# Output products in two matmuls of 256 columns, and moving tiles 128 bytes further on

## The chip, the cores and the metric

The kernel runs on one core of a Trainium2 chip. TensorE (PE) multiplies: a weight load puts a stationary tile of 128 columns into the array, and a matmul streams a moving tile of up to 512 columns past it into one bank of PSUM. VectorE (DVE), ScalarE (ACT) and GpSimd (POOL) work beside it, and DMA queues, issued from SyncE (SP) and POOL, move data between HBM and the on-chip memory SBUF. The metric is the time of one execution in device microseconds (us), the median of several runs.

## The reference

```
q = softmax over the 64 channels; k = softmax over the 576 positions     # 8 batches, 8 heads
kv = k^T v                      # per batch and head, 64 x 64
x  = q kv                       # gathered to 4608 tokens x 512
gate = sigmoid(x @ w_gate);  val = x @ w_val          # 512 x 1536 each
out  = (gate * val) @ w_out                           # 1536 x 512
```

All inputs and the output are float32.

## The kernel before, in words

The 4608 tokens are cut into nine windows w of 512. The first (w = 0) runs in plain float32 (lines 613 and 640) while the weights are still being unpacked, and the other eight run in float32r, where every operand is split into a high and a low part and a product is three matmuls: high by high, high by low, low by high.

A window of these eight takes six steps, and a step has two stages on TensorE that follow each other without a gap:

- `g1(w, p)` computes gate and value for 256 of the 1536 inner columns, by a scheme with seven block products of 12 matmuls each: 84 matmuls, all of 256 columns (line 658). Stationary are weights from `a_w` or `s_sb`, moving are the tiles `c_hl`, made from x. Both halves of the array's input are read from SBUF: 128 columns of weights and 256 columns of moving data for each matmul, and each matmul has a weight load of its own.
- `g2(w, at)` multiplies the step before (256 inner columns) by the output weights into four PSUM banks `acc`: 24 matmuls, before the change of 512 columns (line 726). Stationary is `h`, moving is `wo_hl`.

In the steps of each window but the last, the attention of the next window is woven in. Behind the third `g1`, `k_mm` (line 378) makes k^T v for a batch, in 20 float32 matmuls of 128 columns; it follows `g1` and stands ahead of `g2`. Behind the fifth `g2`, `x_mm` (line 541) multiplies q by kv for the four pairs of heads: 3 matmuls for each part of the window, where a window has two parts if a batch ends in it. The parts are 128 and 384 columns in window 2, 192 and 320 in 3, 256 and 256 in 4, 320 and 192 in 5, 384 and 128 in 6, 448 and 64 in 7, and 512 alone in 8. Moving are tiles of the pool `ring`, stationary is `kv_sb`.

The order on every engine is the order in which the code is written (a manual schedule). Where a tile lies in SBUF follows from the order and the sizes of the pools at the top, with unused tiles (`pad_a`, `pad_w`) that push the later pools on. By this allocation the stationary tiles `a_w`, `s_sb`, `h` and `kv_sb` start at 128 bytes modulo 512 in their partition, and the moving tiles `c_hl`, `wo_hl`, `wo_t`, `x_0` and `ring` at 448 modulo 512. Slices inside them are multiples of 512 bytes away from the start, but for the parts in `x_mm`.

The output weights' next pair (`wo_load`, line 234) and the next sums `s_sb` (`s_load`, line 278) are loaded by DMAs on POOL's queue, each as soon as TensorE has read the tile that it overwrites. So TensorE's pace sets when they start.

Of the kernel before, what the change touches and what calls it, by code (L numbers as in the profile page):

```python
# [8 lines left out]
F32 = mybir.dt.float32  # L9
# [8 lines left out]
P = 128  # L18
# [4 lines left out]
HT = T // 2  # L23
NW = NTOK // T
NT = T // P
NP = H // 2
NJ = DF // P
NK = DM // P
NS = NJ // 2
# [22 lines left out]
def attn_moe(ctx: ExitStack, tc: tile.TileContext, qf, qn, qT, k, kT, v, wg, wv, wo, out):  # L52
    nc = tc.nc

    const = ctx.enter_context(tc.tile_pool(name="const", bufs=1))


    cpool = ctx.enter_context(tc.tile_pool(name="cpool", bufs=1))
    apad = ctx.enter_context(tc.tile_pool(name="apad", bufs=1))
    apool = ctx.enter_context(tc.tile_pool(name="apool", bufs=1))  # L60
    two = ctx.enter_context(tc.tile_pool(name="two", bufs=2))
    wpad = ctx.enter_context(tc.tile_pool(name="wpad", bufs=1))
    wpool = ctx.enter_context(tc.tile_pool(name="wpool", bufs=2))
    four = ctx.enter_context(tc.tile_pool(name="four", bufs=4))
    ring = ctx.enter_context(tc.tile_pool(name="ring", bufs=11))
    small = ctx.enter_context(tc.tile_pool(name="small", bufs=2))
    apad.tile([P, 48], F32, name="pad_a")
    wpad.tile([P, 80], F32, name="pad_w")
    dpool = ctx.enter_context(tc.tile_pool(name="dpool", bufs=2, space=bass.MemoryType.DRAM))
    spool = ctx.enter_context(tc.tile_pool(name="spool", bufs=1, space=bass.MemoryType.DRAM))  # L70
    ps_acc = ctx.enter_context(tc.tile_pool(name="ps_acc", bufs=NT, space=bass.MemoryType.PSUM))
# [451 lines left out]
    def x_parts(w):  # L523
        t0 = w * T
        b0, b1 = t0 // S, (t0 + T - 1) // S
        if b0 == b1:
            return [(b0, 0, T)]
        cut = b1 * S - t0
        return [(b0, 0, cut), (b1, cut, T)]

    def x_mm(w, hp):
        qh, ql = qT_hl.pop((w, hp))
        if w > 1 and hp < 3:
            ps = ps_gv.tile([P, T], F32, name="gv")
        else:
            ps = ps_at.tile([P, T], F32, name="at")
        x_ps[w, hp] = ps
        for b, f, t in x_parts(w):
            kh, kl = (kv_sb[:, b % 2, i, hp] for i in range(2))
            for lh, rh in ((0, qh), (0, ql), (1, qh)):  # L540
                nc.tensor.matmul(  # L541
                    ps[:, f:t], lhsT=kl if lh else kh, rhs=rh[:, f:t],
                    start=(lh == 0 and rh is qh), stop=(lh == 1),
                )

    def x_ev(w, hp):
        copy = nc.vector.tensor_copy if hp % 2 and w > 1 else nc.scalar.copy
# [53 lines left out]
    acc = {}  # L601
# [25 lines left out]
    def acc_new(w):  # L627
        acc[w] = [ps_acc.tile([P, DM], F32, name="acc") for _ in range(NT)]

    def acc_out(w):  # L630
        for m in range(NT):
            nc.scalar.copy(out=x_32[:, m], in_=acc[w][m])
            nc.sync.dma_start(out=out[w * T + m * P:w * T + (m + 1) * P], in_=x_32[:, m])
        del acc[w]
# [79 lines left out]
    def step(w, i):  # L714
        return (i - 1) % NS if w == 1 else i

    def g2(w, at):
        p = step(w, at)
        if at == 0:
            acc_new(w)  # L720
        h, o = h_hl.pop((w, p)), wo_hl.pop((w, p))
        for i in range(2):
            for m in range(NT):
                sl = slice(m * P, (m + 1) * P)
                for lh, rh in ((0, 0), (0, 1), (1, 0)):
                    nc.tensor.matmul(  # L726
                        acc[w][m], lhsT=h[lh][:, i, sl], rhs=o[i][:, rh],
                        start=(at == 0 and i == 0 and lh == 0 and rh == 0),
                        stop=(at == NS - 1 and i == 1 and lh == 1),
                    )  # L730
        if at == NS - 1:
            acc_out(w)

# [42 lines left out]
    def side_b(n, p):  # L776
        if p == 0:
            for hp in range(NP):
                q_spread(n, "m", hp)
        if p == 1:  # L780
            for hp in range(NP):
                qT_load(n, hp)
        if p == 2:
            for hp in range(NP):
                q_spread(n, "r", hp)
        if p == 3:
            for hp in range(NP):
                qT_mul(n, hp)
        if p == 4:
            for hp in range(NP):  # L790
                x_mm(n, hp)
                x_ev(n, hp)
            c_subs()
        load_next(n, p)
# [38 lines left out]
    def after_first(j):  # L833
# [28 lines left out]
        if 6 <= j <= 9:  # L862
            x_mm(1, j - 6)
# [76 lines left out]
    ps = ps_acc.tile([P, DM], F32, name="acc")  # L940
# [5 lines left out]
    m = const.tile([P, NP, 1], F32, name="kmax_0")  # L946
# [115 lines left out]
    for w in range(1, NW):  # L1062
        last = w == NW - 1
        for at in range(NS):
            p = step(w, at)
            end = last and at == NS - 1
            g1(w, p, None if end else step(w + (at + 1) // NS, (at + 1) % NS))
            if at == NS - 1 and not last:
                c_split(0)
                h_split(w, p)  # L1070
                for i in range(1, 7):
                    c_split(i)
            else:
                h_split(w, p)
            if not last:
                side_a(w + 1, at)
            if prev is None:
                g2_0(NJ - 1)
                wo_next(1, 0)
                wo_next(1, 1)  # L1080
            else:
                g2(*prev)
                if not end:
                    wo_next(w + (at + 1) // NS, (at + 1) % NS)
            prev = (w, at)
            if not last:
                side_b(w + 1, at)
    g2(*prev)


# [36 lines left out]
```

## Time and profile before

| | |
|---|---|
| median of 3 runs | 973.95 us (973.04 to 975.06) |
| the profiled execution, its own time | 974.03 us |
| its span, first to last instruction | 972.2 us |
| TensorE matmuls busy | 946.6 us, 97% of the span |
| TensorE weight loads busy | 819.3 us, 84% |
| VectorE, ScalarE, GpSimd busy | 613.2, 488.3, 168.3 us |
| mean granted clock of TensorE | 0.991 of full |

The span lies 1.8 us below the profiled execution's own time, and that time is within 0.1 us of the median, so a saving read off the trace can be taken from either. Matmuls overlap in the array, so the "mean" of a group (279 ns for 256 columns) is how long one is under way, not how far apart two follow. How far apart they follow is read from the chain in order of time, where a stage's length divided by its matmuls is the spacing.

### The profile page before, as it was taken

How to read it: one execution, taken by the hardware profiler on the slowest of the kernel's cores; microseconds unless marked ns; L12 is line 12 of the kernel's file. 1: busy time of each engine (PE TensorE's matmuls, PEld its weight loads, DVE VectorE, ACT ScalarE, POOL GpSimd, SP SyncE). 2: the span in 40 equal slices, each digit the busy share in tenths (PEclk: the TensorE clock that was granted, in tenths of full speed). 3: DMA queues.
4: the chain of work that ended last, by engine and by line, in shares of the span. 5: the costliest groups of instructions: out<-in, count | busy, mean ns of one | idle time of the engine just before them, and what ended most of it. 6: DMA issues, size and time to landing. Idle time of an engine off the chain costs nothing.

```text
span 972.2 us, 15629 instructions
## 1 busy us (share of the span) xinstructions
PE 946.6 (97%) x6062; PEld 819.3 (84%) x6062; DVE 613.2 (63%) x1013; ACT 488.3 (50%) x824; POOL 168.3 (17%) x316
## 2 busy tenths in 40 slices
PE   5899998899999999999999999999999999999998
PEld 4444543699999999999999999999999999999997
DVE  8788878766666566756684667566755655564242
ACT  4689784563456354726472547254635333533222
POOL 0110001221112112111211112111212121212210
PEclk8999999999999999999999999999999999999999
DMA  9986475899699978999899979997999689858672
GB/s 326 350 277 256 178 275 201 292 349 322 197 270 341 303 233 208 383 282 274 184 380 309 269 164 382 317 274 155 370 319 250 208 249 311 240 173 258 200 209 71
DMA packets 93865, 257.79 MB, mean 265 GB/s; under 512 B 15264, under 2 KB 17568, under 8 KB 93024
## 3 DMA queue, kind: packets, MB, share of 16 engines
q0 software_dynamic: 43712, 168.32, 57.5%
q1 hardware_dynamic: 50080, 88.48, 31.3%
q8 instruction: 48, 0.79, 0.4%
q14 instruction: 25, 0.20, 0.1%
HBM read 228.20 MB, written 28.56 MB: 264 GB/s over the span
## 4 chain that ended last, share of the span: by engine, by line
PE 91%; DMA 3%; DVE 2%; ACT 2%; issue 1%; POOL 0%; SPq 0%; POOLq 0%; DVEq 0%; ACTq 0%
PE gv L658 48%; PE acc L726 27%; PE gv L613 6%; PE at L378 3%; PE acc L640 3%; PE gv L541 2%; DMA kmax_row<-k_max 1%; DMA s<-s_sb 1%; PE at L541 1%; DMA s_sb<-s 1%; DMA lent<-k_in 1%; ACT s_sb L265 0%; PE acc L564 0%; ACT f_w L162 0%; DVE a_w L269 0%
## 5 line engine op out<-in xcount | busy, mean ns | idle before, releaser
L658 PE MATMUL gv<-c_hl,s_sb 128*128 128x256 f32 x2304 | 284.6, 279 | 0.3 <-DMA s_sb<-s 0.3
L658 PEld LDWEIGHTS gv<-c_hl,s_sb 128*128 128x128 f32 x2304 | 275.7, 188 | 0.4 <-issue 0.4
L726 PE MATMUL acc<-wo_hl,h 128*128 128x512 f32 x1152 | 272.2, 392 | 0.0
L726 PEld LDWEIGHTS acc<-wo_hl,h 128*128 128x128 f32 x1152 | 213.0, 188 | 44.5
L658 PE MATMUL gv<-c_hl,a_w 128*128 128x256 f32 x1728 | 226.2, 279 | 0.7 <-DVE a_w L269 0.7
L658 PEld LDWEIGHTS gv<-c_hl,a_w 128*128 128x128 f32 x1728 | 214.9, 188 | 5.2 <-issue 1.0
L278 POOL DMA_DIRECT2D s_sb<-s x188 | 100.3, 534 | 314.0 <-PE gv L658 313.9
L684 DVE TENSOR_TENSOR sg<-gv,sg 128x512 f32<-128x512 f32 x48 | 33.2, 691 | 148.5 <-PE gv L658 148.3
L676 ACT COPY sg<-gv 128x512 f32<-128x512 f32 x48 | 28.2, 588 | 148.2 <-PE gv L658 146.5
L234 POOL DMA_DIRECT2D wo_hl<-wo x96 | 51.1, 533 | 297.4 <-PE acc L726 297.3
L686 ACT COPY sg<-gv 128x512 f32<-128x512 f32 x48 | 28.2, 587 | 106.2 <-PE gv L658 106.2
L613 PE MATMUL gv<-x,f_w 128*128 128x512 f32 x160 | 72.3, 605 | 3.5 <-ACT h L621 3.5
L688 DVE TENSOR_TENSOR sg<-sg 128x512 f32<-128x512 f32 x48 | 33.2, 693 | 59.8 <-ACT sg L686 59.8
L613 PEld LDWEIGHTS gv<-x,f_w 128*128 128x128 f32 x160 | 30.5, 193 | 41.3 <-issue 35.8
L709 DVE TENSOR_TENSOR h<-sg,h 128x1024 fp32r<-128x1024 f32 x48 | 58.8, 1226 | 1.6
L697 DVE TENSOR_TENSOR sg<-sg 128x512 f32<-128x512 f32 x48 | 33.3, 693 | 33.5 <-ACT sg L691 33.5
L691 ACT ACTIVATE sg<-sg 128x512 f32<-128x512 f32 x48 | 30.4, 632 | 47.9 <-DVE sg L690 47.9
L640 PE MATMUL acc<-wo_t,h 128*128 128x512 f32 x96 | 44.8, 611 | 5.6 <-DVE h L625 5.6
L681 ACT COPY sg<-gv 128x512 f32<-128x512 f32 x48 | 28.2, 587 | 39.5 <-PE gv L658 39.5
L678 ACT COPY sg<-gv 128x512 f32<-128x512 f32 x48 | 28.2, 587 | 38.6 <-PE gv L658 38.6
L640 PEld LDWEIGHTS acc<-wo_t,h 128*128 128x128 f32 x96 | 18.8, 197 | 29.6 <-issue 21.5
L492 DVE TENSOR_TENSOR ring<-ring,q_b 128x512 f32<-128x512 f32 x28 | 18.6, 691 | 34.9 <-DMA ring<-qT_in 34.8
(152 smaller groups left out, 1050.9 us busy)
## 6 DMA issues: line engine op xcount, KB each, us to landing
s_sb<-s POOLq DMA_DIRECT2D x188, 512.0 KB, 7.4
wo_hl<-wo POOLq DMA_DIRECT2D x96, 512.0 KB, 6.3
s<-s_sb POOLq DMA_DIRECT2D x6, 2048.0 KB, 7.6
out<-x SPq DMA_DIRECT2D x36, 256.0 KB, 9.7
ring<-k_in SPq DMA_DIRECT2D x28, 256.0 KB, 14.5
ring<-qn_in SPq DMA_DIRECT2D x28, 256.0 KB, 9.7
q_b<-q_m_row SPq DMA_DIRECT2D x56, 128.0 KB, 9.6
ring<-qT_in SPq DMA_DIRECT2D x28, 256.0 KB, 9.2
```

The source lines that it names most:

```text
L234: nc.gpsimd.dma_start(out=t.rearrange("p h e -> p (h e)"), in_=wo_dram[2 * p + i].bitcast(F32R))
L278: nc.gpsimd.dma_start(out=s_sb[:, i].rearrange("p h n e -> p (h n e)"), in_=s_dram[p][:, i * n:(i + 1) * n].bitcast(F32R),)
L541: nc.tensor.matmul(ps[:, f:t], lhsT=kl if lh else kh, rhs=rh[:, f:t], start=(lh == 0 and rh is qh), stop=(lh == 1),)
L613: nc.tensor.matmul(ps[n], lhsT=w[:, kt // 2, sl], rhs=x_0[:, kt], start=(kt == 0), stop=(kt == NK - 1),)
L640: nc.tensor.matmul(acc[0][m], lhsT=h_0[j][:, m * P:(m + 1) * P], rhs=wo_t[j // 2][:, j % 2], start=(j == 0), stop=(j == NJ - 1),)
L658: nc.tensor.matmul(ps[:, n], lhsT=lh(kt), rhs=c_hl[i][:, x, kt], start=(first and n == 0 and kt == 0 and lh is wh and x == 0), stop=(last ...
L684: nc.vector.tensor_tensor(out=sg[:, 0], in0=rr, in1=sg[:, 0], op=ALU.add)
L688: nc.vector.tensor_tensor(out=sg[:, 3], in0=sg[:, 3], in1=sg[:, 2], op=ALU.add)
L691: nc.scalar.activation(sg[:, 0:2, 0], sg[:, 0:2, 0], AF.Sigmoid)
L697: tt(out=sg[:, 0:2, 0], in0=sg[:, 0:2, 0], in1=sg[:, 0:2, 1], op=ALU.mult)
L709: nc.vector.tensor_tensor(out=lo, in0=sg[:, :, 0], in1=hi.bitcast(F32), op=ALU.subtract)
L726: nc.tensor.matmul(acc[w][m], lhsT=h[lh][:, i, sl], rhs=o[i][:, rh], start=(at == 0 and i == 0 and lh == 0 and rh == 0), stop=(at == NS - ...
```

## The change

Three edits. In `g2` each matmul of 512 columns becomes two of 256 columns, with the same stationary tile, into the two halves of the same bank: 24 become 48 in a stage, 1152 become 2304 in all, and each of the second ones has a weight load of its own. In the pools, a tile of 32 words ahead of `cpool` moves `c_hl` (and `x_0`) by 128 bytes, from 448 to 64 modulo 512; `pad_a` shrinks by the same 32 words, so `a_w` and `h` stay; `pad_w` grows by 32 words, so that `wo_hl` (and `wo_t`) move from 448 to 64; a new `pad_f` of 96 words brings the pools behind it, `ring` among them, back to 448. In `x_mm`, for the last of the four pairs of heads alone, the parts are sorted so that one of 128 to 256 columns comes last, and where the last part is wider than 256 columns its last matmul is cut in two.

```
+    cpad = ctx.enter_context(tc.tile_pool(name="cpad", bufs=1))
     cpool = ctx.enter_context(tc.tile_pool(name="cpool", bufs=1))
...
     wpool = ctx.enter_context(tc.tile_pool(name="wpool", bufs=2))
+    fpad = ctx.enter_context(tc.tile_pool(name="fpad", bufs=1))
     four = ctx.enter_context(tc.tile_pool(name="four", bufs=4))
...
-    apad.tile([P, 48], F32, name="pad_a")
-    wpad.tile([P, 80], F32, name="pad_w")
+    cpad.tile([P, 32], F32, name="pad_c")
+    apad.tile([P, 16], F32, name="pad_a")
+    wpad.tile([P, 112], F32, name="pad_w")
+    fpad.tile([P, 96], F32, name="pad_f")
...
-        for b, f, t in x_parts(w):
+        parts = x_parts(w)
+        if w > 1 and hp == NP - 1:
+            parts.sort(key=lambda x: (P <= x[2] - x[1] <= HT, x[2] - x[1]))
+        for b, f, t in parts:
             kh, kl = (kv_sb[:, b % 2, i, hp] for i in range(2))
             for lh, rh in ((0, qh), (0, ql), (1, qh)):
-                nc.tensor.matmul(
-                    ps[:, f:t], lhsT=kl if lh else kh, rhs=rh[:, f:t],
-                    start=(lh == 0 and rh is qh), stop=(lh == 1),
-                )
+                cuts = [f, t]
+                if w > 1 and hp == NP - 1 and lh and b == parts[-1][0] and t - f > HT:
+                    cuts.insert(1, (f + t) // 2)
+                for f0, t0 in zip(cuts, cuts[1:]):
+                    nc.tensor.matmul(
+                        ps[:, f0:t0], lhsT=kl if lh else kh, rhs=rh[:, f0:t0],
...
                 for lh, rh in ((0, 0), (0, 1), (1, 0)):
-                    nc.tensor.matmul(
-                        acc[w][m], lhsT=h[lh][:, i, sl], rhs=o[i][:, rh],
...
+                    for e in range(2):
+                        es = slice(e * HT, (e + 1) * HT)
+                        nc.tensor.matmul(
+                            acc[w][m][:, es], lhsT=h[lh][:, i, sl], rhs=o[i][:, rh, es],
```

On TensorE's order, the first place is the step of window 1 in which `k_mm` (into `at`) stands between `g1` (into `gv`) and `g2` (into `acc`). Before:

```order
L658 MATMUL gv<-c_hl,a_w 128x256 x12
L378 MATMUL at<-v_104,ring 128x128 x4
L378 MATMUL at<-v_105,ring 128x128 x4
L378 MATMUL at<-f_last,ring 128x128 x12
L726 MATMUL acc<-wo_hl,h 128x512 x24
```

The same place now:

```order
L670 MATMUL gv<-c_hl,a_w 128x256 x12
L382 MATMUL at<-v_112,ring 128x128 x4
L382 MATMUL at<-v_113,ring 128x128 x4
L382 MATMUL at<-f_last,ring 128x128 x12
L740 MATMUL acc<-wo_hl,h 128x256 x48
```

Nothing moves here; the 24 matmuls of 512 columns are 48 of 256, so from `k_mm` on all that follows is 256 columns wide.

The second place is the attention of window 7 on TensorE, the end of `x_mm` (the last pair of heads goes to `at`) and the stages around it. Before:

```order
L726 MATMUL acc<-wo_hl,h 128x512 x24
L541 MATMUL gv<-ring,kv_sb 128x448 x3
L541 MATMUL gv<-ring,kv_sb 128x64 x3
...
L541 MATMUL at<-ring,kv_sb 128x448 x3
L541 MATMUL at<-ring,kv_sb 128x64 x3
L658 MATMUL gv<-c_hl,a_w 128x256 x12
```

The same place now:

```order
L740 MATMUL acc<-wo_hl,h 128x256 x48
L552 MATMUL gv<-ring,kv_sb 128x448 x3
L552 MATMUL gv<-ring,kv_sb 128x64 x3
...
L552 MATMUL at<-ring,kv_sb 128x64 x3
L552 MATMUL at<-ring,kv_sb 128x448 x2
L552 MATMUL at<-ring,kv_sb 128x224 x2
L670 MATMUL gv<-c_hl,a_w 128x256 x12
```

In the last pair of heads the 64 columns now come first, and the third matmul of 448 columns is two of 224, so that `g1` follows on a matmul of 224 columns and not of 64. In windows 2 and 3 the narrower part (128, 192) comes last instead of the wider one; in 8 the third matmul of 512 is two of 256; 4, 5 and 6 stay as they are.

## Rows read from the trace of the kernel before

**Rows 1.** The page's first part: busy time, share of the span, instructions.

```profile
PE 946.6 (97%) x6062; PEld 819.3 (84%) x6062; DVE 613.2 (63%) x1013; ACT 488.3 (50%) x824; POOL 168.3 (17%) x316
```

**Rows 2.** The page's chain that ended last, by line, shares of the span.

```profile
PE gv L658 48%; PE acc L726 27%; PE gv L613 6%; PE at L378 3%; PE acc L640 3%; PE gv L541 2%; DMA kmax_row<-k_max 1%; DMA s<-s_sb 1%; PE at L541 1%; DMA s_sb<-s 1%; DMA lent<-k_in 1%; ACT s_sb L265 0%; PE acc L564 0%; ACT f_w L162 0%; DVE a_w L269 0%
```

**Rows 3.** Waits: who for whom, total us, times, longest.

```profile
POOL s_sb L278 <- PE gv L658: 313.9, 185, 6.1
POOL wo_hl L234 <- PE acc L726: 297.3, 92, 8.5
...
PE gv L658 <- DMA s_sb<-s: 0.3, 1, 0.3
```

**Rows 4.** The chain in order of time: start us, length us, what.

```profile
178.72 9.94 PE gv L658 x82
...
195.18 7.31 PE gv L658 x60
202.48 5.51 PE acc L726 x24
207.99 9.52 PE gv L658 x84
217.51 4.66 PE at L378 x40
222.17 5.71 PE acc L726 x24
227.88 9.89 PE gv L658 x84
...
418.50 4.66 PE at L378 x40
423.16 5.72 PE acc L726 x24
428.88 9.52 PE gv L658 x84
438.40 5.49 PE acc L726 x24
443.89 9.52 PE gv L658 x84
458.90 2.04 PE gv L541 x18
460.94 0.68 PE at L541 x6
461.62 9.52 PE gv L658 x84
...
641.96 9.52 PE gv L658 x84
...
660.36 9.94 PE gv L658 x84
670.30 5.51 PE acc L726 x24
675.80 9.52 PE gv L658 x84
...
947.65 9.89 PE gv L658 x84
957.55 11.00 PE acc L726 x48
```

**Rows 5.** Two stages of g1 by windows: stretch, length, busy; clock is third from the right.

```profile
428.70:438.20 9.50, 9.50 (x85) 9.48 (x84) 6.04 (x13) 2.75 (x5) 2.66 (x5) 1.00 1.21 251
526.40:536.30 9.90, 9.90 (x86) 9.90 (x85) 7.60 (x15) 2.85 (x5) 2.67 (x5) 1.00 1.20 320
```

**Rows 6.** Timeline of TensorE at one k_mm: start us, length us, what.

```profile
516.02 1.95 PE L378 MATMUL at<-v,ring 128*128 128x128 f32 x16
517.81 3.04 PE L378 MATMUL at<-f_last,ring 128*128 128x128 f32 x24
```

More of the change, by code (lines that the diff above doesn't have):

```diff
@@ L537, in x_mm @@
         x_ps[w, hp] = ps
-        for b, f, t in x_parts(w):
+        parts = x_parts(w)
+        if w > 1 and hp == NP - 1:
+            parts.sort(key=lambda x: (P <= x[2] - x[1] <= HT, x[2] - x[1]))
+        for b, f, t in parts:
             kh, kl = (kv_sb[:, b % 2, i, hp] for i in range(2))
             for lh, rh in ((0, qh), (0, ql), (1, qh)):
-                nc.tensor.matmul(
-                    ps[:, f:t], lhsT=kl if lh else kh, rhs=rh[:, f:t],
-                    start=(lh == 0 and rh is qh), stop=(lh == 1),
-                )
+                cuts = [f, t]
[4 more added lines that the diff above has]
+                        ps[:, f0:t0], lhsT=kl if lh else kh, rhs=rh[:, f0:t0],
+                        start=(lh == 0 and rh is qh), stop=(lh == 1),
+                        skip_group_check=True,
+                    )
     def x_ev(w, hp):
@@ L725, in g2 @@
                 for lh, rh in ((0, 0), (0, 1), (1, 0)):
-                    nc.tensor.matmul(
-                        acc[w][m], lhsT=h[lh][:, i, sl], rhs=o[i][:, rh],
-                        start=(at == 0 and i == 0 and lh == 0 and rh == 0),
-                        stop=(at == NS - 1 and i == 1 and lh == 1),
-                    )
+                    for e in range(2):
+                        es = slice(e * HT, (e + 1) * HT)
+                        nc.tensor.matmul(
+                            acc[w][m][:, es], lhsT=h[lh][:, i, sl], rhs=o[i][:, rh, es],
+                            start=(at == 0 and i == 0 and lh == 0 and rh == 0 and e == 0),
+                            stop=(at == NS - 1 and i == 1 and lh == 1 and e == 1),
+                            skip_group_check=True,
+                        )
         if at == NS - 1:
```

## Prediction

> **What bounds the kernel now.** I read the page's first part first: TensorE's matmuls are busy for 946.6 of 972.2 us [rows 1]. The chain that ended last says the same by line: 75% of the span is the two stages that the change touches, 48% `g1` (L658) and 27% `g2` (L726) [rows 2]. The waits show that nothing holds these two up: matmuls of `g1` waited 0.3 us in all for `s_sb`, while POOL, which issues the loads of `s_sb` and `wo_hl`, stood 313.9 and 297.3 us waiting for TensorE [rows 3]. So the time is the number of matmuls times their spacing, and the question is what the change does to the spacing.
>
> The chain in order of time gives the spacing stage by stage [rows 4], and there the reader should see something odd. A stage of `g1` is always the same 84 matmuls, yet it takes either 9.52 us (113.3 ns each) or 9.89 us (117.7 ns), and nothing between. Of the 46 full stages from 207.99 to 947.65, 12 take 9.52 and 34 take 9.89 to 9.97. The granted clock is 1.00 in either kind, and matmuls and weight loads are both busy all the time [rows 5], so it is neither the clock nor a wait: TensorE falls into a fast or a slow step and keeps it. The change of step is seen at three places only: across `k_mm` and the `g2` behind it (from 9.90 at 408 to 9.52 at 428 us, and from 9.52 at 208 to 9.89 at 228 us), across `x_mm` with unequal parts (9.52 at 642, 9.94 at 660), and across one `g2` behind that (9.94 at 660, 9.52 at 676) [rows 4]. Across `x_mm` of window 4, which is 256 columns throughout, the fast step holds: 18 matmuls in 2.04 us are 113.3 ns, and `g1` behind takes 9.52 [rows 4]. Each place where the step changed has matmuls wider than 256 columns in it or next behind it.
>
> A stage of `g2` takes 5.49 to 5.51 us in either step, 5.71 behind `k_mm`, and the last two together 11.00: 229 ns for 512 columns [rows 4].
>
> **The change part by part.** *Twice the output matmuls.* 1152 matmuls at 229.0 ns become 2304 of the very shape of `g1`'s (256 columns, a weight load of 128 for each). Their price is bounded by `g1`'s two steps: a pair costs 2 x 113.3 = 226.7 ns in the fast one, 2 x 117.7 = 235.5 in the slow one. Over 1152 products that is 2.7 us gained or 7.4 us lost, and the extra weight loads are in these prices. The floor that I can read for a matmul that is no longer than its weight load is `k_mm`: 16 matmuls from 516.02 to 517.81 us are 111.9 ns each [rows 6]. It is float32 and another shape, so it bounds the price from below and no more.
>
> A rule speaks against this part. The Trainium skill, "TensorE: Matmul & The Clock Gate", Back-to-back issue gap, gives columns divided by 2.4 plus 2.5 ns, 109.2 ns for 256 and 215.8 for 512, so that splitting a product would cost 2.6 ns, 3.0 us in all and an estimated 977. The rows show both shapes slower than that, and in the fast step two matmuls of 256 columns (226.7) are cheaper than one of 512 (229.0), so the sum goes by the rows.
>
> *No more 512s behind k_mm.* With the widest matmuls gone from `g2`, what moved the step between stages is mostly gone, so a step once taken should be kept from one `k_mm` or `x_mm` to the next. This can cut both ways: fast everywhere turns 34 slow stages into 9.52, 34 x 0.37 = 12.6 us, and the two first stages (82 matmuls in 9.94 us and 60 in 7.31, 121 and 122 ns with their pauses, so no faster than the slow step) add 142 x 4.4 ns, 0.6; slow everywhere turns the 12 of 9.52 into 9.89, a loss of 12 x 0.37 = 4.4 us.
>
> *Moving tiles at 64 instead of 448 modulo 512.* No row has float32r moving tiles at 64 with weights at 128, so its price is not in the trace. Its bounds are `g1`'s two steps, and below them the 111.9 ns. [...] I take the fast step: it is the row for 256 columns following on 256 columns (window 4), which is what nearly all of the program becomes. What speaks for the slow one is that all starts after a pause led to it at 448: the first `g1` at 178 us, on which two slow stages and then 5.51 of `g2` followed [rows 4]. With the address as it was I would have called slow the likelier.
>
> *The attention's end.* It reorders 3 matmuls in two windows or three, and adds one matmul in windows 7 and 8 each: nothing beyond 0.2 us by itself, as one matmul costs 113 to 118 ns. What it can be worth is the step in which the next `g1` starts, counted above.
>
> *What could uncover.* A step of the window would last 9.52 + 5.44 = 14.96 us, where the shortest now lasts 15.01 (428.88 to 443.89) [rows 4]. So loads never get a shorter time than they have now in the stretch from 428 us, where the chain runs through TensorE alone; that cover holds, and I add nothing.
>
> **The sum.** From the profiled execution's 974.03 us: 12.6 + 0.6 for `g1`, 2.7 for `g2`, together 15.9, so 958.1; I say 958. The fast step may miss a window (each has six stages of `g1`, and six of `g2` at 24 pairs x 8.8 ns = 0.2, so 6 x 0.37 + 6 x 0.2 = 3.5 us), and it may be a little better than 113.3: with all 6,336 matmuls of both stages at 111.9 it is another 8.9 us, 949. The range of this case is 947 (the floor, less the 2 us by which three runs differ) to 968 (three windows slow).
>
> **The rivals.** *Slow everywhere (the other side).* The chain of 256 columns settles in the slow step, because the fresh start behind every `k_mm` and `x_mm` leads there, and without 512s nothing leads out: 4.4 + 7.4 = 11.8 us lost, 986. For it speaks what followed the first start; against it the moved address and the fast passage through window 4. It decides from the first stages on: if they take 9.89 and `g2` 5.65, everything will. The point at which it costs as much as it gains is where g1 and g2 together break even: with a share f of stages fast, the sum is 34 x 0.37 + 0.6 + 2.7 less (1 - f) times 27.7 us (the distance between the two ends), so that below f = 0.43 the kernel is slower than before.
>
> *The address does nothing, and the steps fall as before.* A quarter of the stages fast (12 of 46), so that a product of 512 columns costs 2 x (12 x 113.3 + 34 x 117.7)/46 = 233.1 ns: 1152 x 4.1 = 4.7 us lost, 979. For it: the steps before fell without any sign of a rule that I can read off `x_mm`, whose parts start at other addresses. The Trainium skill, "SBUF — State Buffer", Who interferes with whom, states that TensorE's two read ports are independent and that TensorE waits on nobody, by which addresses would be worth nothing. The trace does not agree that nothing is lost there: one shape, two spacings, no wait.
>
> *The change does not do what it says for the most part.* The step is fast in about half of the windows, gain and loss cancel, and the time is within 0.2% of before (2 us), which is about what a measurement of this kernel can tell from no change: 972 to 976.
>
> **How the numbers follow.** Fast nearly everywhere, at 113.3 ns or better: 0.60, of which 0.1 for spacings at or near the floor. Cancelling: 0.08. Steps as before: 0.12. Slow everywhere: 0.20. So faster 0.60, same 0.08, slower 0.32. The likeliest time is 958. As three cases in ten end above the old time, the range has to reach to the slow end: 947 to 987.
>
> **What would show it.** Right: in the chain in order of time, 84 matmuls of `g1` in 9.5 us in nearly all 46 stages, among them those behind `k_mm` and behind the attention of unequal parts; `g2` with 48 matmuls in 5.4 us; the number of weight loads larger by 1152 and busy nearly as long as the span of these stages; TensorE still waiting for nobody. Wrong: stages of 9.89 from the start on, `g2` at 5.65; or a step that still changes from window to window, which would put the cause into `k_mm` and `x_mm` and not into the 512s. A new spacing below 113 or above 118 would say that the address set the size itself, not only which step is taken.

## The result

| | before | after |
|---|---|---|
| median, six runs each | 975.33 us | 964.94 us (963.35 to 970.11) |
| ratio, with its 95% interval | | 0.9904 (0.9878 to 0.9931) |
| the profiled execution | 974.03 us | 964.64 us |
| its span | 972.2 us | 962.9 us |

The kernel became 1% faster: 10.4 us between the medians, 9.4 between the two profiled executions. That is the side that was forecast and 6 to 7 us short of the size (958). One of the six executions took 970.11 us, 3.4 above the next; it has no trace, so which of its stages were long is not known. I call the two spacings of the prediction the short step (113.3 ns) and the long one (117.7 ns).

The page's first part of the changed kernel answers to [rows 1]: TensorE's instructions grow by 1154 of either kind (1152 in `g2`, and one each in the attention of windows 7 and 8), and weight loads are busy for 89% of the span instead of 84.

```profile
PE 939.4 (98%) x7216; PEld 859.7 (89%) x7216; DVE 613.7 (64%) x1013; ACT 487.7 (51%) x824; POOL 167.0 (17%) x316
```

The chain in order of time (start us, length us, what) answers to [rows 4]. L670 is `g1` now, L740 `g2`, L382 `k_mm`, L552 `x_mm`.

```profile
203.77 5.44 PE acc L740 x48
209.21 9.68 PE gv L670 x84
218.89 4.66 PE at L382 x40
223.55 5.66 PE acc L740 x48
229.20 9.52 PE gv L670 x84
...
261.70 0.81 PE at L552 x6
262.50 9.58 PE gv L670 x84
272.08 5.44 PE acc L740 x48
...
836.50 5.44 PE acc L740 x48
...
844.01 0.69 PE at L552 x4
844.70 9.89 PE gv L670 x84
854.59 5.65 PE acc L740 x48
...
937.98 9.89 PE gv L670 x84
947.87 11.32 PE acc L740 x96
```

The reader should see that 39 of the 46 stages of `g1` now take 9.52 us (up to 9.68 with a short gap at their start or in them), where 12 did before; among the 39 are those behind `k_mm` and behind the attention of unequal parts. `g2` takes 5.44 instead of 5.49 to 5.51: 48 matmuls at 113.3 ns. Then, behind the attention of window 8, everything goes over to 9.89 and 5.65 and stays there to the end. So this kernel shows both steps too, at one address and one width.

The windows of a `g1` of either step (length, then busy us of PE, PEld, DVE, ACT and POOL; granted clock third from the right) show again that it is not the clock, and that TensorE's matmuls and its weight loads are busy all the time in both. They answer to [rows 5].

```profile
440.00:449.52 9.52, 9.52 (x86) 9.52 (x86) 3.36 (x6) 5.15 (x11) 2.65 (x5) 1.00 1.05 349
860.24:870.14 9.90, 9.90 (x87) 9.90 (x86) 3.88 (x6) 3.00 (x6) 2.65 (x5) 1.00 0.69 202
```

The waits answer to [rows 3]: TensorE still waits 0.3 us in all for `s_sb`, and POOL for TensorE.

```profile
POOL s_sb L282 <- PE gv L670: 301.9, 183, 6.0
...
PE gv L670 <- DMA s_sb<-s: 0.3, 1, 0.3
```

### The profile page after: what moved, and what is told of

Its sections match the earlier page's. It is cut to its first block, busy times and chain, and to the rows that moved or that the text cites. A ratio compares the mean times of both kernels' runs of the same rounds, so it can differ in the third digit from the quotient of the medians.

```text
span 962.9 us, 17939 instructions
## 1 busy us (share of the span) xinstructions
PE 939.4 (98%) x7216; PEld 859.7 (89%) x7216; DVE 613.7 (64%) x1013; ACT 487.7 (51%) x824; POOL 167.0 (17%) x316
## 4 chain that ended last, share of the span: by engine, by line
PE 90%; DMA 4%; DVE 2%; ACT 2%; issue 1%; POOL 0%; SPq 0%; POOLq 0%; DVEq 0%; ACTq 0%
PE gv L670 47%; PE acc L740 27%; PE gv L625 6%; PE at L382 3%; PE acc L652 3%; PE gv L552 2%; DMA s<-s_sb 2%; DMA kmax_row<-k_max 1%; PE at L552 1%; DMA s_sb<-s 1%; DMA lent<-k_in 1%; PE gv L507 0%; DVE s_sb L273 0%; ACT s_sb L269 0%; PE acc L576 0%
## 5 line engine op out<-in xcount | busy, mean ns | idle before, releaser
L670 PE MATMUL gv<-c_hl,s_sb 128*128 128x256 f32 x2304 | 278.8, 277 | 0.3 <-DMA s_sb<-s 0.3
L740 PE MATMUL acc<-wo_hl,h 128*128 128x256 f32 x2304 | 271.2, 277 | 0.0
L670 PEld LDWEIGHTS gv<-c_hl,s_sb 128*128 128x128 f32 x2304 | 270.1, 188 | 0.6 <-issue 0.5
L740 PEld LDWEIGHTS acc<-wo_hl,h 128*128 128x128 f32 x2304 | 266.4, 188 | 0.7
L670 PE MATMUL gv<-c_hl,a_w 128*128 128x256 f32 x1728 | 221.5, 277 | 0.0
L670 PEld LDWEIGHTS gv<-c_hl,a_w 128*128 128x128 f32 x1728 | 207.9, 188 | 1.0 <-issue 1.0
```

What stands on the lines that cost most here:

```text
L670: nc.tensor.matmul(ps[:, n], lhsT=lh(kt), rhs=c_hl[i][:, x, kt], start=(first and n == 0 and kt == 0 and lh is wh and x == 0), stop=(last ...
L740: nc.tensor.matmul(acc[w][m][:, es], lhsT=h[lh][:, i, sl], rhs=o[i][:, rh, es], start=(at == 0 and i == 0 and lh == 0 and rh == 0 and e == 0),
```

## The experiments

Four theories stood against each other. **Mine**: matmuls wider than 256 columns (the 512s of `g2` above all) knock TensorE from one step into the other, and the addresses decide into which step it settles after a pause. **A**: the address alone sets the spacing. **S**: the width alone does, and addresses are nothing. And beside these, that the attention's end does nothing. All medians stand beside runs of the kernel before on the same chip; stages are counted in the profiled execution.

### One part at a time

**Addresses alone.** From the changed kernel, the matmuls of `g2` are 512 columns again and `x_mm` is as before.

```
...
-                            acc[w][m][:, es], lhsT=h[lh][:, i, sl], rhs=o[i][:, rh, es],
+                        acc[w][m], lhsT=h[lh][:, i, sl], rhs=o[i][:, rh],
...
```

> Only the pools move: c_hl and wo_hl at 64 modulo 512, output products of 512 columns and the attention as before. My theory (512s knock the step, the address only decides which step a start settles in): stages of g1 of both lengths, 9.52 and 9.89 us, changing behind g2 or the attention, 966 to 980 us in all. Rival A (the address alone sets the spacing): 9.52 in all 46 stages, about 961 to 964. Rival S (the width alone, the address is nothing): about a quarter of the stages at 9.52, 974 to 976.

Measured: 971.90 us against 975.13, ratio 0.997 (0.9957 to 0.9983). The chain in order of time has 31 stages of `g1` at 9.53 to 9.61 and 15 at 9.89, and the step changes again and again:

```profile
207.89 9.53 PE gv L662 x84
217.42 4.66 PE at L382 x40
222.07 5.79 PE acc L730 x24
227.87 9.89 PE gv L662 x84
...
262.28 9.89 PE gv L662 x84
272.17 5.60 PE acc L730 x24
277.77 9.53 PE gv L662 x84
```

A does not hold: the address alone leaves both steps. Nor does S, which expected a quarter of the stages short. The `g2` at 272 us shows what the 512s do: 9.89 in front of a `g2` of 512 columns, 9.53 behind it. A side result is that 512 columns are dearer at this address, 5.59 us or 233 ns, against 229 in [rows 4]: 48 stages of 0.09 us give back 4.

**Split alone.** Old pads, old `x_mm`, `g2` in 256 columns.

> Only the output products are split into 256 columns; all addresses and the attention as before. My theory: behind every pause the step settles at 117.7 ns at this address, g1 at 9.89 and g2 at 5.65 nearly throughout, 983 to 987 us. Rival A: as my theory. Rival S: mostly 9.52 and 5.44, with windows 2, 3 and 8 at 9.89 because their attention ends wide, 968 to 972.

Measured: 987.98 us, ratio 1.0134 (1.0110 to 1.0158). All 46 stages of `g1` are long (9.89 to 9.97), and every `g2` is at 5.65 or, behind `k_mm`, 5.85:

```profile
230.49 9.89 PE gv L658 x84
240.38 5.65 PE acc L728 x48
```

S falls here again: the width alone makes the kernel slower, by about what the prediction's first rival had worked out (986), and 1 us more than I expected at most.

**Split and attention's end, old addresses.** The changed kernel with the old pads.

```
-    cpad.tile([P, 32], F32, name="pad_c")
-    apad.tile([P, 16], F32, name="pad_a")
-    wpad.tile([P, 112], F32, name="pad_w")
-    fpad.tile([P, 96], F32, name="pad_f")
+    apad.tile([P, 48], F32, name="pad_a")
+    wpad.tile([P, 80], F32, name="pad_w")
```

> Split and the attention's end, all addresses as before (448). My theory: the step settles at 117.7 ns behind pauses, 9.89 and 5.65 nearly throughout, 982 to 987 us. Rival S (width and attention's end do it, the address is nothing): as with the whole change, 963 to 967.

Measured: 987.18 us, ratio 1.0124 (1.0109 to 1.0139), all 46 stages long:

```profile
229.97 9.89 PE gv L666 x84
```

This and the changed kernel run the same instructions in the same order; unused pads of 16 to 112 words are 22 us.

**Split and addresses, old attention.** The changed kernel with the old `x_mm`.

> Split and address, the attention ends as before (384 columns in window 2, 320 in 3, 512 in 8, 64 in 7). My theory: 9.52 and 5.44 where the attention ends on 256 columns or fewer and behind every k_mm, 9.89 and 5.65 in the steps behind the wide ends of windows 2 and 3 up to the next k_mm, and in window 8: 965 to 970 us. Rival (the attention's end does nothing): the same as with the whole change, 963 to 966, stage by stage.

Measured: 972.09 us, ratio 0.9968 (0.9958 to 0.9979), so with the other two parts in place the attention's end is worth 7 us. 25 stages are short; the long ones are behind the attention of windows 2, 3, 7 and 8, up to the next `k_mm` or, behind 7 and 8, to the end. Around window 2:

```profile
242.55 9.52 PE gv L662 x84
...
260.09 0.86 PE at L545 x6
260.95 9.89 PE gv L662 x84
270.84 5.65 PE acc L732 x48
...
307.58 9.89 PE gv L662 x84
317.48 4.66 PE at L382 x40
322.13 5.66 PE acc L732 x48
327.79 9.52 PE gv L662 x84
```

The attention ends there on 384 columns, and the long step follows; `k_mm`, with its 128 columns, brings the short one back. Windows 2, 3 and 8 were expected. Window 7 was a miss: there the attention ends on 64 columns, and what follows is long as well (9.97, then 9.89), so the time is 2 us above the range I had given.

```profile
753.63 0.94 PE at L545 x6
754.57 9.97 PE gv L662 x84
```

It is no rule that such an end leads into the long step. In the run with the addresses alone the same attention, at the same addresses, is followed by a short stage; there the `g2` in front of it was still of 512 columns, and whether that makes the difference is open:

```profile
759.87 0.95 PE at L545 x6
760.81 9.61 PE gv L662 x84
```

### Window 8

The last pair's third matmul is cut into four of 128 columns instead of two of 256; all else as in the changed kernel.

```
-                    cuts.insert(1, (f + t) // 2)
+                    cuts = list(range(f, t + 1, P)) if t - f == T else [f, (f + t) // 2, t]
```

> The whole change, but in window 8 the third matmul of the last pair of heads is cut into four of 128 columns instead of two of 256. If a narrower end lets the next g1 settle in the step of 113.3 ns: window 8 at 9.52 and 5.44 instead of 9.89 and 5.65, 7 x 0.37 + 8 x 0.21 = 4.3 us less than the whole change, 960 to 961.5. If the 512s before it decide: stages as in the whole change, 964 to 966.

Measured: 960.75 us (960.02 to 961.42), ratio 0.9856 (0.9836 to 0.9875), faster than both kernels. The end of its chain, where the changed kernel had 9.89, 5.65 and 11.32:

```profile
844.86 0.85 PE at L552 x6
845.71 9.57 PE gv L670 x84
855.28 5.44 PE acc L740 x48
...
945.04 10.89 PE acc L740 x96
```

Two more matmuls, 0.16 us, win seven stages of `g1`, six of `g2` and the last two. In this execution window 1 began in the long step instead (9.89 at 209.55 us) and was put right by the first `k_mm`, while in the changed kernel it began in the short one (9.68 at 209.21): the same addresses, and the same program up to window 8. So TensorE can start in either step, and no run shows what decides it.

### Which addresses

Here the expectations rest on what had been seen by then: 448 long, 64 short.

**Everything 128 bytes further on**, moving tiles at 64 and stationary at 256, with the split alone.

```
+    const.tile([P, 32], F32, name="pad_k")
     s_sb = const.tile([P, 4, 2, 2, 2 * P], F32R, name="s_sb")
```

> As the kernel with the split alone (old pads, old end of the attention), but everything lies 128 bytes further on, so moving tiles are at 64 and stationary ones at 256 modulo 512: the distance between the two is that of before. If the distance counts: g1 at 9.89 and g2 at 5.65 throughout, 986 to 989 us, as with the split alone. If the moving tile's own address counts: 9.52 and 5.44 in most stages, 965 to 973 us.

Measured: 985.97 us, ratio 1.0117 (1.0093 to 1.0141), all 46 stages long, `g2` at 5.65:

```profile
228.65 9.89 PE gv L659 x84
```

With stationary tiles at 128, moving tiles at 64 and the old attention, 25 stages were short (972.09 us). So it is the distance of the moving tile from the stationary one that counts, not its own address, as far as one run with other stationary addresses can show it.

**Moving tiles at 192 and at 320.** The pads `c, a, w, f` are 64, 112, 16, 64 and 96, 80, 48, 32 words.

> The whole change with c_hl and wo_hl at 192 instead of 64 modulo 512 (64 bytes behind the stationary tiles' 128 instead of 64 ahead). If addresses matter modulo 256 only, as the attention's parts at 256 bytes' distance suggest: as at 448, so 9.89 and 5.65 nearly throughout, 986 to 988 us. If it is modulo 512: open between 960 and 988, and other than at 448.

> The whole change with c_hl and wo_hl at 320 modulo 512. If addresses matter modulo 256 only: as at 64, so 9.52 and 5.44 but in window 8, 963 to 967 us. If it is modulo 512: other stages than at 64, up to 988 us.

Measured: 986.49 us at 192, ratio 1.0122 (1.0097 to 1.0148), all 46 long:

```profile
228.38 9.89 PE gv L670 x84
```

And 963.63 us at 320, ratio 0.9888 (0.9862 to 0.9913), with 39 short and the seven of window 8 long, as at 64:

```profile
229.08 9.52 PE gv L670 x84
...
844.47 9.89 PE gv L670 x84
```

So 256 bytes more change nothing: the distance counts modulo 256.

**Moving tiles at 128, 0 and 96**, all three from the version with window 8 mended (960.75 us). The pads `c, a, w, f` are 48, none, none, 80; 16, 32, 96, 112; and 40, 8, 120, 88 words.

> As the version with the 128-column cut in window 8 (960.75 us), but c_hl and wo_hl at 128 modulo 512, where the stationary tiles start too (distance 0). Known by now: distances of 64 modulo 256 settle at 117.7 ns, 192 modulo 256 at 113.3. If half of the 256 bytes is long and the other half short, with 0 on the long side: 9.89 and 5.65 throughout, 986 us. If only 64 is bad: as 960.75. A third spacing would say that the distance sets the size as well.

> As the version with the 128-column cut in window 8 (960.75 us), but c_hl and wo_hl at 0 modulo 512 (distance 128 modulo 256). If the half from 128 to 255 is short: 9.52 and 5.44, about 961 us. If only 192 is good: 9.89 and 5.65, 986. A third spacing would say that the distance sets the size as well.

> As the version with the 128-column cut in window 8 (960.75 us), but c_hl and wo_hl at 96 modulo 512: distance 224 modulo 256, half way between the good 192 and the worst one measured, 0 (120.0 ns). If the spacing follows the distance smoothly: between 113.3 and 120 ns, g1 at about 9.8 us, 975 to 985. If blocks of 64 bytes count: as at 64, 960 to 962. If 192 is not yet the best: g1 below 9.5, under 960.

Measured: 1001.71 us at 128, ratio 1.0274 (1.0250 to 1.0298); 994.22 at 0, ratio 1.0197 (1.0175 to 1.0219); 990.56 at 96, ratio 1.0170 (1.0137 to 1.0203). The chains have new lengths. At 128:

```profile
231.32 10.08 PE gv L666 x84
```

At 0:

```profile
246.19 9.97 PE gv L670 x84
```

At 96:

```profile
228.87 9.94 PE gv L670 x84
```

So the distance sets the size of the step too, which the prediction had named as a thing to look for (a spacing above 118 ns). The guess that half of the 256 bytes is short was wrong, as was the one that 0 is as bad as 64; and 96, for which I expected at most 985, is close to the other long ones (118.3 ns) and not half way between 113.3 and 120.0. All these runs moved `c_hl` and `wo_hl` together, so none tells which of the two decides.

### The attention's own tiles

`ring` at 64 as well, by leaving `pad_f` out, from the version with window 8 mended.

```
-    fpad.tile([P, 96], F32, name="pad_f")
```

> As the version with the 128-column cut in window 8 (960.75 us), but ring, the attention's moving tiles, at 64 modulo 512 too (distance 192 from kv_sb). If the distance rule holds for the attention as well: window 4's 24 matmuls at 113.3 instead of 117.7 ns, 0.1 us, and the same steps behind it elsewhere: 960 to 961, not to be told from 960.75. If the attention's own step carries over into g1: stages of 9.89 appear behind some windows.

Measured: 969.00 us, ratio 0.9943 (0.9928 to 0.9957), 8 us dearer by the medians than with `ring` at 448 (960.75), and 5.3 by the profiled executions (966.73 and 961.42 us). I had looked for long stages behind the attention; they came behind `k_mm`, in four of its six places:

```profile
315.63 4.66 PE at L380 x40
320.29 5.85 PE acc L738 x48
326.14 9.89 PE gv L668 x84
```

`ring` holds the stationary tiles of `k_mm`, and moving it changes in which step what follows begins. So the new `pad_f`, which looks like tidying, is worth 5 to 8 us here, and the start behind `k_mm` depends on its addresses as well as on `g2`'s.

The same trace shows what the attention's end does when it finds TensorE in the long step. Windows 3, 6 and 7, which end on 192, 128 and 224 columns, led out of it; window 4, of 256 columns throughout, left it as it was:

```profile
351.58 5.65 PE acc L738 x48
...
360.31 9.55 PE gv L668 x84
...
450.69 5.65 PE acc L738 x48
...
459.17 9.89 PE gv L668 x84
```

## Why the prediction was right

**The spacing is what changed.** From 203.77 us on the chain is TensorE's, as before; no wait came up, and the two lengths of a stage are the two that the prediction read off before. That a step once taken is kept when the 512s are gone held too: in the changed kernel no `g2` of these stages changes the step, and it changes only across `x_mm` of window 8. The prediction saw the step change before at three kinds of places and missed a fourth: it took the two first stages as slow, and behind them stand 5.51 us of `g2` and then 9.52 of `g1` [rows 4]. So the step also changed across a `g2` of 512 columns with no attention ahead of it, which fits its mechanism.

**The address decides which step, and the side was partly luck.** The prediction had no row for 64 and took the short step because 256 columns following on 256 had kept it in window 4. That reason did not carry: at the old addresses the same stream of 256 columns is long in all 46 stages, at 987 to 988 us against the rival's 986. That much the prediction had granted, since at 448 it called the long step the likelier. What made 64 good was not known, and of the other four distances that were run none settled at 113.3 ns. The Trainium skill, "SBUF — State Buffer", Who interferes with whom, has TensorE's two read ports independent and TensorE wait on nobody. If the starts of its own two operands were worth nothing by that, the runs do not agree, since 22 us hang on them; that the ports are the place of it no run shows.

**The size.** The sum was 15.9 us, and the profiled executions differ by 9.4, so 6.5 are missing. The terms that were too large are 34 x 0.37 and `g2`'s 2.7, both of them taken for all windows: window 8 stayed long. There 7 stages of 0.37 and 6 of 0.21 are lost, and the last two stages of `g2` take 11.32 instead of 10.89 (that end measured with window 8 mended): 2.6 + 1.3 + 0.4 = 4.3 us. The version that mends just that window is 4.2 us faster, so this is shown. Short gaps at the start of `g1` or within it (9.68 at 209 us, 9.58 behind the attention, and the like) sum to 0.5. To the two first stages the sum gave 0.6; instead the first `g2` of window 1 starts 1.3 us later, at 203.77 and not at 202.48. In the other runs it starts anywhere from 201.97 to 204.88, so this is spread. Together that is 4.3 + 0.5 + 1.9 = 6.7 us, within 0.2 of what is missing.

**The attention's end** was put at nothing beyond 0.2 us by itself, which holds for the matmuls that it adds, and its effect on the next `g1` was named but given no price of its own. Taken out of the changed kernel alone it costs 7 us (972.09 against 964.94), where taking out the addresses costs 22 (987.18).

**The rule on narrow matmuls.** The 3.0 us that the prediction worked out by a formula were not the page's price for this kernel: the Trainium skill, "TensorE: Matmul & The Clock Gate", Back-to-back issue gap, gives that formula for a single matmul by itself, and says that in a stream of weight loads and matmuls both set the spacing. Here two matmuls of 256 columns take 226.7 ns where one of 512 took 229, as the sum had it, and only at a good address; at 448 a pair takes 235.5.

**The rivals.** The long step everywhere was real, with its size, and is the same kernel without the new pads. Gains and losses nearly cancel where a part is missing (971.90 with the addresses alone, 972.09 without the attention's end). Steps falling as before, a quarter of them short, were seen in no run.

What stays open is the mechanism. Shown are that the start address matters, by its distance modulo 256 from the stationary tile, and that what ran before decides which of two steps is kept. Where in the chip this arises no run tests. Why two of 256 columns behind 512s end in the long step and four of 128 do not is settled only so far: with `ring` at 64, an attention of 256 columns kept the long step, and ends on 128, 192 and 224 led out of it.

## What to carry to other kernels

When a stage of the same matmuls takes two different times in one trace at one clock and without a wait, look at which stages come before each, and at where the stationary and the moving operand start in SBUF: here 128 bytes are 22 of 987 us. A change of widths and a change of addresses have to be tried together: here the addresses alone won 3 us, the width alone cost 13, and the two with the attention's end won 10. And look at the few places where wider or narrower matmuls break the stream: one matmul cut into four instead of two was worth 4 us over a whole window.

## What the runs showed of the hardware that I had not expected

In these runs, with float32r operands, matmuls of 256 columns and a weight load of 128 for each, the spacing depends on the start of the moving tile less that of the stationary one, modulo 256 bytes (from the stage of 84 matmuls; stationary tiles at 128, or 256 in one run of the second row):

| distance | spacing that it settles at | seen with moving tiles at |
|---|---|---|
| 0 | 120.0 ns (10.08 us) | 128 |
| 64 | 117.7 ns (9.89 us) | 448, 192, and 64 with stationary at 256 |
| 128 | 118.7 ns (9.97 us), in some stretches 120.0 | 0 |
| 192 | 113.3 ns (9.52 us), or 117.7 where wider matmuls, and once 64 columns, led into it | 64, 320 |
| 224 | 118.3 ns (9.94 us) | 96 |

At distance 64 the short step exists too (12 stages before), but only behind a `g2` of 512 columns did these traces change into it. At 192 both are kept once taken, over seven stages and more. Attention that ends on 320, 384 or 512 columns was followed by the long one each time; ends on 128, 192 or 224 by the short one, also out of the long one; an end on 256 by either, and one on 64 by either (9.97 and 9.61 us in two runs). At 192 the wide matmuls are dearer than at 64: 233 against 229 ns for 512 columns.
